# Three 1 MB stores split into 124 and 4 partitions, in a kernel for the gradients of one-query attention

## The chip, the cores and the metric

One core of one Trainium2 chip. The metric is the device time of one execution in microseconds (us); lower is better. Runs whose core shows the usual clock are called fast runs and only these are compared. Every comparison has runs of the kernel before on the same chip beside it.

## The reference, cut to what matters

```python
B, H, Sq, Skv, Dh = 1, 32, 1, 8192, 128            # all bfloat16

def _fwd_reference(q, k, v):
    scores = jnp.einsum('bhqd,bhkd->bhqk', q, k) * q.shape[-1] ** -0.5
    attn = jax.nn.softmax(scores, axis=-1)
    return jnp.einsum('bhqk,bhkd->bhqd', attn, v)

def reference(q, k, v, grad_out):
    out, vjp = jax.vjp(_fwd_reference, q, k, v)
    return (out, *vjp(grad_out))                    # out, dQ, dK, dV
```

With one query per head, K and V (2 MB a head each) are read once, and dK and dV (2 MB a head each) are written once. That is 134 MB in and 134 MB out. dV of a head is an outer product: p (8192 numbers) times grad_out (128 numbers).

## The kernel before

All large transfers are issued by one queue (SP). A tile has 128 partitions; partition p holds 64 neighbouring rows of the sequence, so that half a tile of dK or dV is one contiguous piece of 8 KB a partition. K and V are loaded whole, with 16 KB a partition. dK and dV are written in halves of 1 MB:

```python
    def rows_of(x, h, c, parts):
        L = NT // parts
        return x[0, h].rearrange("(p n) d -> p n d", p=P)[:, c * L:(c + 1) * L, :]

    def load_k(h):
        Kt[h] = kpool.tile([P, NT, D], BF16, tag="K", name="Kt")
        parts = NCH if h == 0 else 1
        for c in range(parts):
            nc.sync.dma_start(slots(Kt[h], c, parts), rows_of(k, h, c, parts))
    # ... load_v is the same with V
    # ... outer(h, which, r): quarter r of dK or dV of head h
        nc.vector.tensor_tensor(slots(G, r, 4)..., op=ALU.mult)
        parts = 4 if h == H - 1 else NST            # NST = 2
        if r % (4 // parts) == 4 // parts - 1:
            c = r // (4 // parts)
            nc.sync.dma_start(rows_of(dst, h, c, parts), slots(G, c, parts))
    # ... the loop over heads, cut to the order of the transfers
    for h in range(H + 1):
        p_ = h - 1
        # ... load_v(h + 1); ds_of(p_); outer(p_, "dk", 0); dq_of(p_, 0)
        if h > 0:
            dq_of(p_, 1)
            outer(p_, "dk", 1)                      # stores the first half of dK
        if 0 < h and h + 2 < H:
            load_k(h + 2)
        # ... outer(p_, "dk", 2), outer(p_, "dk", 3): second half of dK; then both halves of dV of h
```

## Time and profile before

| kernel before | value |
|---|---|
| median of 3 runs | 667.95 us (667.87 to 668.68) |
| busiest compute engine | 77% (PE, DVE) |
| share of the span in which the 16 transfer engines had packets of the large transfers | 97.0% |
| bytes moved, from the page | 134 MB read and 134 MB written |

The prediction below shows the lines of the profile that this rests on: the engine line, the row of GB/s in 40 slices of the span, the share of the large queue, the chain of waits, three stretches of time, the waits of the issuing queue and the landing times of the transfers.

### The profile page before, as it was taken

The numbers are of one execution on the slowest core, as the hardware profiler recorded it, in microseconds if no ns is written. First come the engines' busy times: TensorE is split into PE (matmuls) and PEld (weight loads), VectorE is DVE, ScalarE is ACT, GpSimd is POOL, SyncE is SP. The second block draws the span as 40 slices with busy tenths as digits, with TensorE's granted clock in tenths as the row PEclk, the third lists the DMA queues.
The fourth block names the chain that finished last, engine by engine and source line by source line (L and its number), as shares of the span: only waits on it lengthen the run. The fifth ranks groups of instructions, "written<-read, shape, count | busy, mean of one in ns | idle before, by whom it ended". The sixth has DMA issues, their size and how long they took to land.

```text
span 667.0 us, 23105 instructions
## 1 busy us (share of the span) xinstructions
PE 516.8 (77%) x10727; PEld 485.8 (73%) x10727; DVE 512.5 (77%) x658; ACT 182.1 (27%) x321; POOL 0.7 (0%) x6
## 2 busy tenths in 40 slices
PE   2887988888887777878779787787776888778881
PEld 1887878878877767877668676677766777677870
DVE  4797888888877797777877778777788776887762
ACT  0333323232323222232222322223312223223230
POOL 0000000000000000000000000000000000000000
PEclk9995556566565565555555655666557665555555
DMA  8999999999999999999999999999999999999783
GB/s 330 414 425 424 419 427 414 424 423 426 425 425 424 425 425 424 425 429 423 423 427 426 423 416 422 413 412 418 395 423 418 397 416 406 409 420 403 270 357 142
DMA packets 29807, 269.94 MB, mean 405 GB/s; under 512 B 3472, under 2 KB 3472, under 8 KB 6032
## 3 DMA queue, kind: packets, MB, share of 16 engines
q1 hardware_dynamic: 29712, 268.48, 97.0%
q8 instruction: 83, 1.36, 0.7%
q14 instruction: 12, 0.10, 0.0%
HBM read 134.23 MB, written 134.23 MB: 403 GB/s over the span
## 4 chain that ended last, share of the span: by engine, by line
DMA 75%; PE 17%; DVE 3%; ACT 2%; issue 1%; SPq 0%; ACTq 0%
DMA Kt<-in_k_dram 26%; DMA Vt<-in_v_dram 26%; DMA out_dram<-G_dv 23%; PE T_ps L168 7%; PE s_ps L145 2%; PE dp_ps L185 2%; PE m_ps L185 2%; PE dp_ps L180 1%; DVE XK_sb L133 1%; ACT XT_sb L170 1%; PE m_ps L255 1%; DVE G_dk L195 1%; PE m_ps L268 1%; PE s_ps L161 0%; ACT qd L211 0%
## 5 line engine op out<-in xcount | busy, mean ns | idle before, releaser
L168 PE MATMUL T_ps<-ident,Vt 128*128 128x128 bf16 x2048 | 228.7, 302 | 31.9 <-DMA Vt<-in_v_dram 31.9
L168 PEld LDWEIGHTS <-Vt 128*128 128x128 bf16 x2048 | 201.1, 142 | 33.8 <-DMA Vt<-in_v_dram 33.6
L133 DVE STREAM_TRANSPOSE XK_sb<-Kt 128x1024 f32<-128x1024 f32 x128 | 148.2, 1213 | 81.1 <-DMA Kt<-in_k_dram 81.1
L170 ACT COPY XT_sb<-T_ps 128x1024 f32<-128x1024 f32 x128 | 129.5, 1012 | 189.7 <-PE T_ps L168 189.7
L195 DVE TENSOR_TENSOR G_dk<-ds_rep,qd 128x2048 bf16<-128x2048 bf16 x128 | 155.7, 1219 | 1.1
L195 DVE TENSOR_TENSOR G_dv<-p_rep,qd 128x2048 bf16<-128x2048 bf16 x128 | 148.2, 1220 | 8.5 <-ACT p_rep L277 8.5
L180 PEld LDWEIGHTS <-XT_sb 128*128 128x128 bf16 x2048 | 74.7, 106 | 27.2 <-ACT XT_sb L170 27.2
L180 PE MATMUL dp_ps<-doT,XT_sb 128*128 128x1 bf16 x2048 | 73.6, 166 | 24.4 <-ACT XT_sb L170 24.4
L145 PE MATMUL s_ps<-q_blk,XK_sb 128*128 128x4 bf16 x2048 | 59.1, 168 | 23.2 <-DVE pdt L216 20.5
L145 PEld LDWEIGHTS <-XK_sb 128*128 128x128 bf16 x2048 | 56.5, 103 | 25.5 <-DVE pdt L216 22.3
L185 PE MATMUL dp_ps<-ds_rep,Kt 128*128 128x1 bf16 x2048 | 64.7, 165 | 6.6 <-issue 6.0
L185 PEld LDWEIGHTS <-Kt 128*128 128x128 bf16 x2048 | 59.9, 104 | 12.3 <-issue 12.3
L185 PEld LDWEIGHTS <-Vt 128*128 128x128 bf16 x2048 | 61.1, 105 | 0.0
L185 PE MATMUL m_ps<-p_rep,Vt 128*128 128x1 bf16 x2048 | 60.5, 166 | 0.0
L226 ACT COPY dq_all<-dp_ps 128x1 f32<-128x1 f32 x32 | 5.1, 159 | 173.9 <-PE dp_ps L185 173.9
L268 PEld LDWEIGHTS m_ps<-rs,ones_f 128*128 128x128 f32 x64 | 16.0, 310 | 48.6 <-ACT e L267 48.6
L268 PE MATMUL m_ps<-rs,ones_f 128*128 128x1 f32 x64 | 18.7, 360 | 39.2 <-ACT e L267 39.2
L264 DVE TENSOR_REDUCE nbias<-m_ps 128x1 f32<-128x128 f32 x32 | 9.3, 292 | 22.0 <-ACT qd L211 22.0
L255 PE MATMUL m_ps<-diag,ones_f 128*128 128x128 f32 x64 | 25.3, 499 | 0.7 <-DVE diag L253 0.7
L218 DVE SCALAR_TENSOR_TENSOR ds_rep<-dp_ps,pdt,p_s 128x256 bf16<-128x256 f32 x32 | 15.5, 484 | 12.0 <-PE dp_ps L180 9.6
L277 ACT ACTIVATE p_rep<-e,rinv 128x256 bf16<-128x256 f32 x32 | 16.2, 507 | 30.3 <-DVE rinv L275 30.3
L211 ACT CAST qd<-m_ps 128x256 bf16<-128x256 f32 x32 | 11.9, 372 | 42.4 <-PE m_ps L207 42.4
(40 smaller groups left out, 163.0 us busy)
## 6 DMA issues: line engine op xcount, KB each, us to landing
Kt<-in_k_dram SPq DMA_DIRECT2D x31, 2048.0 KB, 28.0
out_dram<-G_dv SPq DMA_DIRECT2D x62, 1024.0 KB, 25.8
out_dram<-G_dk SPq DMA_DIRECT2D x62, 1024.0 KB, 28.0
Vt<-in_v_dram SPq DMA_DIRECT2D x30, 2048.0 KB, 28.3
Vt<-in_v_dram SPq DMA_DIRECT2D x8, 512.0 KB, 13.8
Kt<-in_k_dram SPq DMA_DIRECT2D x4, 512.0 KB, 5.4
out_dram<-G_dv SPq DMA_DIRECT2D x4, 512.0 KB, 16.9
out_dram<-G_dk SPq DMA_DIRECT2D x4, 512.0 KB, 10.7
```

Of the source, the lines that this page charges most:

```text
L133: nc.vector.transpose(XK[h][:, :, :, u, :], slots(Kt[h], u, NCH).rearrange("p g d -> p (g d)").bitcast(F32).rearrange("p (g w j) -> p g w ...
L145: nc.tensor.matmul(out[:, g, :], lhsT=cols[:, g, c // 2, c % 2], rhs=q_blk[:, h, c, :], start=(c == 0), stop=(c == 2 * NB - 1), skip_group ...
L168: nc.tensor.transpose(T_ps[:, i, :], Vt[h][:, c * CH + i, :], ident[:])
L170: nc.scalar.copy(X.rearrange("p c s -> p (c s)").bitcast(F32), T_ps.rearrange("p c s -> p (c s)").bitcast(F32))
L180: nc.tensor.matmul(st[h]["dp"][:, n:n + 1], lhsT=X[:, i, :], rhs=doT[:, h:h + 1], start=True, stop=True, skip_group_check=True)
L185: nc.tensor.matmul(out_col, lhsT=Xt[:, n, :], rhs=rep[:, n, 0:1], start=(n == 0), stop=(n == NT - 1), skip_group_check=True)
L195: nc.vector.tensor_tensor(slots(G, r, 4).rearrange("p n (a b) -> p n a b", b=R), slots(rep, r, 4).unsqueeze(2).to_broadcast([P, Q, D // R, ...
L211: nc.scalar.copy(x["qd"][:].rearrange("p a d -> p (a d)"), x["m"][:, 256:512])
L218: nc.vector.scalar_tensor_tensor(out=x["ds"][:], in0=x["dp"][:, 0:NT].unsqueeze(2).to_broadcast([P, NT, R]), scalar=pdt[:], in1=x["p_s"][: ...
L255: nc.tensor.matmul(x["m"][:, 128:256], lhsT=ones_f[:], rhs=diag[:], start=True, stop=True, skip_group_check=True)
L268: nc.tensor.matmul(x["m"][:, 0:1], lhsT=ones_f[:], rhs=rs[:], start=True, stop=True, skip_group_check=True)
L277: nc.scalar.activation(x["p"][:], e[:].unsqueeze(2).to_broadcast([P, NT, R]), ACT.Copy, scale=rinv[:])
```

## The change

The store of the second half of dV of heads 8, 16 and 24 is cut into 124 and 4 partitions. Point 1 of the prediction says how many engines a transfer uses: as many, up to 16, as divide its partitions. Both pieces, of 124 (4 x 31) and of 4: four engines. So the other twelve have nothing to do in this store. The intent: if one of the twelve sets the end of the kernel, it gets three stores less.

```diff
+SHIFTED = (8, 16, 24)
...
         if r % (4 // parts) == 4 // parts - 1:
             c = r // (4 // parts)
-            nc.sync.dma_start(rows_of(dst, h, c, parts), slots(G, c, parts))
+
+            cuts = (0, P - 4, P) if which == "dv" and h in SHIFTED and c == 1 else (0, P)
+            for lo, hi in zip(cuts, cuts[1:]):
+                nc.sync.dma_start(rows_of(dst, h, c, parts)[lo:hi], slots(G, c, parts)[lo:hi])
```

In what follows, "shifted store" is a store cut in this way.

## The prediction

> **What bounds the kernel now.** I read the page first: engines, slices, chain. The engine lines and the chain:
>
> ```profile
> PE 516.8 (77%) x10727; PEld 485.8 (73%) x10727; DVE 512.5 (77%) x658; ACT 182.1 (27%) x321; POOL 0.7 (0%) x6
> ...
> GB/s 330 414 425 424 419 427 414 424 423 426 425 425 424 425 425 424 425 429 423 423 427 426 423 416 422 413 412 418 395 423 418 397 416 406 409 420 403 270 357 142
> ...
> q1 hardware_dynamic: 29712, 268.48, 97.0%
> ...
> DMA 75%; PE 17%; DVE 3%; ACT 2%; issue 1%; SPq 0%; ACTq 0%
> ```
>
> No compute engine is above 77%, while the data queue has packets in flight for 97.0% of 16 engines' span and the chain that ended last is DMA for 75%. So transfers set the time. The second thing to see is the slope inside the GB/s row: 425 in the first half, 395 to 420 later, with nothing new in the program. The stretches confirm it (columns: stretch, length, busy us of PE, PEld, DVE, ACT, POOL, clock, DMA share, GB/s):
>
> ```profile
> 150.00:250.00 100.00, 81.24 (x1679) 76.39 (x1677) 81.27 (x102) 28.25 (x50) 0.00 (x0) 0.57 1.01 426
> ...
> 450.00:550.00 100.00, 75.90 (x1606) 71.67 (x1607) 76.50 (x95) 27.78 (x49) 0.00 (x0) 0.60 1.01 411
> 550.00:610.00 60.00, 47.58 (x941) 44.72 (x938) 45.57 (x58) 16.95 (x30) 0.00 (x0) 0.53 1.01 413
> ```
>
> Same share, fewer bytes: packets take longer late in the run. Then the issuing queue's waits and the issues:
>
> ```profile
> SPq L203 <- DMA out_dram<-G_dk: 111.7, 52, 2.5
> SPq L203 <- DMA Kt<-in_k_dram: 110.8, 26, 5.2
> SPq L75 <- DMA Vt<-in_v_dram: 97.5, 23, 4.5
> ```
>
> ```profile
> Kt<-in_k_dram SPq DMA_DIRECT2D x31, 2048.0 KB, 28.0
> out_dram<-G_dv SPq DMA_DIRECT2D x62, 1024.0 KB, 25.8
> ```
>
> A store of dK or dV (L203) has no data reason to wait for a load of K. In the trace's issue records only eight completion semaphores are used in turn, so issue n waits until issue n-8 has landed everywhere. Eight issues are about 11 MB, hence some 28 us from issue to landing though 1 MB moves in 2.5 us.
>
> That is an average over 16 engines. The views don't part them, so I took the trace's own records: each transfer's semaphore gets 16 increments, one per engine, each with its time. For a dV store issued at 274.7 us the 16 landings lie, after the first at 286.2 us: seven within 2.6 us, eight from 5.9 to 8.0 us, one at 14.3 us. At 19 us of the run the spread was 0.8 us; at 445 us it is 20.5 us and then stays between 20 and 22. So three kinds of engine exist:
> - seven fast ones;
> - eight that lose about 1.5 us at each 16 KB instruction block: one block took 1009 ns and the packet after it 1106 ns in place of 611; following back-to-back packets, these blocks go round eight engines, about one in 55 us each;
> - one slow one, which gets no such blocks but whose 8 KB packets (stores) take about 315 to 390 ns instead of 309.
>
> The slow engine sets the time. It always has work; the other fifteen run ahead of it until the window of eight issues is used up (445 us), and then wait for it, which is the falling GB/s. At the end it is still alone: the last large store landed on the first engine at 658.3 us and on the last at 665.7 us.
>
> **What the Trainium skill says.**
> 1. "DMA: Bandwidth & Descriptors", section "Why a DMA increments its semaphore by 16 and not by 1": a transfer uses the largest number of engines up to 16 that divides its slowest dimension, and on this issue path the lowest-numbered ones. 128 partitions give 16 (the trace has 16 landings for each transfer); 124 = 4 x 31 gives 4, and 4 gives 4. So both pieces, and not only the small one, move on engines 0 to 3. No transfer of the kernel before uses fewer than 16, so its trace can't show it.
> 2. Same page, "Latency and other measured facts": engines 7 and 15 are usually slower than the rest in traces. The page blames a path that this kernel doesn't use and calls that a guess. The trace agrees that one engine is slower, but doesn't tell its number.
> 3. "Runtime: NRT & Kernel Launch", "Instruction fetch mechanics": each sequencer refills its instruction memory by its own DMA queue in 16 KiB blocks. The trace agrees: 83 packets, 1.36 MB on the instruction queue.
> 4. "SBUF — State Buffer", "Door 1: The DMA port swizzle": a port serves eight given partitions; in a 128-partition transfer each engine has a port to itself. With 31 partitions on one engine that is no longer so. No run so far shows what it costs.
>
> **The change part by part.** Arithmetic, buffers and the instructions of PE, DVE and ACT stay. SP has three more issues, 0.4 us each, on an engine that mostly waits: nothing. The three affected stores, 1 MB each, are at heads 8, 16 and 24.
> - *Off engines 4 to 15:* eight 8 KB packets per store. On a fast engine 8 x 305 ns (309 less 4 of overlap) = 2.44 us; on the slow one 8 x 0.33 = 2.65 us. Three stores: 7.3 and 7.9 us.
> - *Onto engines 0 to 3:* 31 + 1 packets instead of 8, so 24 more: 24 x 305 ns = 7.3 us per store, 22.0 us for three.
> - *The balance.* The slow engine loses (14.3 - 0.8) us over the 267 us from 19 to 286 us, 5.1%. Unthrottled that is, at 640 us, 0.8 + 0.051 x 621 = 32 us behind a fast one (estimate). Engines 0 to 3, if fast, end 22.0 us behind a fast one; the slow engine ends 32 - 7.9 = 24 us behind. So it stays the last, just, and the end moves with its own work: 667.95 - 7.9 = 660.0 us.
> - *In between.* After head 8 (about 180 us) engines 0 to 3 are 7.3 us back, about where the slow one is. After head 24 (about 510 us) they are 22.0 us back and the slow one about 0.8 + 0.051 x 490 - 7.9 = 18 us: for a while they land last, but they have a window of 20 us in front of them, so the slow engine doesn't starve.
> - *Pieces on foreign ports.* While engines 0 to 3 work off the shifted megabyte, the others mostly load (V, then half a dK store, then K), so reads of one port meet seldom. I add 1 us. That gives 661 us. The tail moves with the slow engine, whose backlog lasts to the end.
>
> **The rivals.**
> - *Engines 0 to 3 are among the eight with instruction blocks.* These are about 7.2 us back at 286 us, 2.7%, so 16 to 17 us at 640 us. Plus 22.0 that is 38.5 us against the 32 us of the slow engine now: about 6 us longer, 674 us. Against it: three stores is just the number that balances fast engines against the slow one (7.3n = 32 - 2.65n gives n = 3.2), while for this group it would be under two; whoever chose three seems to have had fast engines. For it: eight of sixteen engines have the blocks, and nothing numbers them. I give it 1 in 5.
> - *Engines 0 to 3 include the slow one, or all 16 are equally the bound.* Then 22 us are added in full: 690 us, 3.3% slower. It is what anyone gets who takes the mean of 97% for every engine. The spread of landings speaks against equality; the page's 7 and 15 against the slow one being below 4. 1 in 10.
> - *A new wait eats the gain.* The load of V after a shifted store lands late because engines 0 to 3 land late, or ports collide heavily: engines 0 to 3 have only about 2 us in hand at the end, so a collision cost of 2 us per store would make them the last engines, at 664 to 668 us. Likely enough to widen the range upward.
> - *More than counted.* If what slows the slow engine is tied to the stores themselves, it gains more than 8 us; beyond 11 us engines 0 to 3 take over, so under 656 us is hard to reach.
>
> **Range and chances.** Some two chances in three lie between 657 and 667 us, around 661; the fetch-group rival at 674 is to be held too, so the range is 657 to 675 us. Faster by over 2% means under 654.6 us, for which both sides of the balance would have to be wrong: 3%. Slower by over 2% means over 681.3 us, the second rival and some unknown: 12%. Within 2%: 85%.
>
> **What would show it.** Right: GB/s stays at about 425 for longer than before and the late stretch 450 to 550 us is above 411; the spread of landings grows to 20 us later than 445 us; each 124-partition store has landings from four engines only and takes about 9.5 us of their time; the last landing on the last engine comes some 7 us earlier. Wrong: the spread of the landings jumps up by 7 us at each of heads 8, 16 and 24 and never falls (then engines 0 to 3 were not ahead); or 8 KB packets of 500 ns and more around these stores (ports); or 16 landings for a 124-partition store (then nothing moved and the time stays at 668).

## The result, and the profile after

| | median | lowest to highest | fast runs |
|---|---|---|---|
| before | 667.91 us | 667.60 to 668.68 | 4 |
| after | 674.65 us | 673.50 to 675.67 | 4 |

The ratio is 1.0099, with a 95% interval of 1.0077 to 1.0120. A ratio is always the mean time of one kernel's fast runs over that of the other's of the same rounds, so it is not quite the ratio of the medians. The outputs of both kernels are correct. The kernel became 6.7 us slower where a gain of 7 us had been forecast.

The page of the kernel after, in the same parts as shown of before:

```profile
PE 511.6 (76%) x10727; PEld 480.9 (71%) x10727; DVE 512.4 (76%) x658; ACT 182.1 (27%) x321; POOL 0.7 (0%) x6
...
GB/s 333 417 421 422 428 418 424 425 422 427 426 403 409 422 425 426 425 426 424 430 404 386 347 428 421 430 425 423 425 429 340 358 292 422 425 423 424 315 405 159
...
q1 hardware_dynamic: 29688, 268.48, 96.1%
...
DMA 70%; PE 20%; DVE 5%; ACT 2%; issue 1%; SPq 0%; ACTq 0%
```

The compute engines have the same work. What is new is three dips in GB/s, one after each shifted store: slight in slices 12 and 13, and deep in 21 to 23 and in 31 to 33. Between them the rate is 420 to 430, also late in the run, where before had fallen to 395 to 420. So the slow decline is gone, and something worse has come in two places.

The same stretches (columns as before: stretch, length, busy us of PE, PEld, DVE, ACT and POOL, clock, DMA share, GB/s), after:

```profile
150.00:250.00 100.00, 80.24 (x1634) 75.48 (x1633) 79.09 (x100) 27.63 (x50) 0.00 (x0) 0.57 1.01 419
330.00:400.00 70.00, 45.55 (x978) 42.60 (x975) 47.08 (x61) 16.43 (x30) 0.00 (x0) 0.60 0.96 392
450.00:550.00 100.00, 69.73 (x1462) 64.95 (x1459) 73.87 (x94) 24.09 (x46) 0.00 (x0) 0.55 0.93 379
550.00:610.00 60.00, 47.44 (x1001) 44.50 (x999) 44.58 (x58) 16.90 (x30) 0.00 (x0) 0.56 1.01 422
```

And the second one of before, which the prediction doesn't show:

```profile
330.00:400.00 70.00, 56.57 (x1157) 53.62 (x1156) 52.03 (x65) 20.08 (x34) 0.00 (x0) 0.53 1.01 423
```

423 GB/s became 392 around the second shifted store, and the DMA share fell under 1: engines stand empty. The prediction had said that the stretch 450 to 550 would be above the 411 of before if it was right. It is 379.

Who stands empty, and why, is in the waits of the issuing queue (total us, times, longest us): the whole run after, then the stretch 330 to 400 alone, then the corresponding line of before.

```profile
SPq L82 <- DMA out_dram<-G_dv: 69.4, 23, 12.4
```

```profile
SPq L82 <- DMA out_dram<-G_dv: 14.4, 2, 12.4
```

```profile
SPq L81 <- DMA out_dram<-G_dv: 55.8, 25, 2.9
```

L82 is the load of V. It waits eight issues behind a shifted store. The longest such wait grew from 2.9 to 12.4 us: the shifted store lands so late that the window of eight issues is used up. In this time the issuing queue starts nothing, and the engines that are ahead run dry.

The issues after, with KB each and the median us from issue to landing on all engines:

```profile
out_dram<-G_dv SPq DMA_DIRECT2D x59, 1024.0 KB, 24.4
...
out_dram<-G_dv SPq DMA_DIRECT2D x3, 992.0 KB
...
out_dram<-G_dv SPq DMA_DIRECT2D x3, 32.0 KB
```

Three stores of 992 KB and three of 32 KB are there. They have no landing time since the view wants 16 landings. In the records, each of the six has landings from four engines.

### The landings, engine by engine

The views don't part the engines, so I worked the following from the trace's landing records. For each transfer of 128 partitions I added up what one engine had been given by all such transfers so far, at 305 ns per 8 KB (the short stores of 124 and 4 and the eight 512 KB loads at the start are left out), and subtracted this sum from each landing time. An engine that does nothing else and never pauses stays at its number. An engine that works a shifted store off rises by the full cost of that store. The fast group rises only if it has to pause. The records don't name an engine, so engines are followed by their place in the order. Shown are the first engine and the last five (us).

```
                        first | the last five
before, near 176 us      15.2 | 19.8 19.9 20.1 20.5 23.9
        near 372 us      15.4 | 24.3 24.4 24.4 26.4 35.0
        near 544 us      24.0 | 30.5 31.3 32.7 33.4 45.1

after,  near 176 us      14.9 | 19.6 19.7 20.1 20.4 22.7     before the first shifted store
        near 203 us      14.9 | 24.7 27.1 28.1 29.9 30.4     after it
        near 332 us      15.0 | 27.2 28.2 30.6 31.1 31.4
        near 364 us      19.8 | 31.6 37.9 40.1 45.3 46.0     after the second
        near 505 us      29.0 | 37.8 39.6 40.2 47.3 48.6
        near 536 us      35.5 | 39.3 53.2 53.6 61.0 63.1     after the third
```

Before, one engine drifts away from the rest, 23.9 to 45.1: the slow one. After, four others rise in three steps, and the slow one (24.7, 31.6, 37.8, 39.3) isn't among them and ends in front of them. Before the first step none of the four stood out. Seven engines stood in front of the others then (within 1.1 us), and three are left there after it: the four come from the front group. So engines 0 to 3 are four of the seven fast ones, and the slow engine is elsewhere, just as the prediction had taken it.

But each step is 14.5 to 15.5 us for the last of the four, from about 15 to 30.4, 31 to 46.0 and 48.6 to 63.1, where 32 packets x 305 ns = 9.8 us had been taken. Between the steps the last engine hardly moves (46.0 to 48.6 in 140 us): it is never without work. It is the one that sets the end.

The packets show the same. 8 KB packets of the large queue that took 420 ns or more, and by how much they exceeded 309 ns in sum, in the 40 us around each shifted store:

```
                    180-220 us        340-380 us        500-540 us
before              2,  0.8 us        6,  2.2 us        4,  1.6 us
after              48, 16.8 us       22,  9.0 us       30, 12.0 us
```

In before such packets are next to absent. In after they take 9 to 17 us in each place, which is 2 to 4 us for each of four engines, if all of them belong to engines 0 to 3; a packet's record doesn't name its engine. The landings allow a check: by the table, the four engines together rise by some 54 to 56, 48 and 55 us at the three stores, which is 15 to 17, 9 and 16 us above 4 x 9.8. That is near the excess of the slow packets at the first two and 4 us more at the third. Of the 48, 14 took 590 to 625 ns, twice the usual time; the longest took 1366 ns.

### The profile page after: what moved, and what is told of

Its sections match the earlier page's. It is cut to its first block, busy times and chain, and to the rows that moved or that the text cites. A ratio compares the mean times of both kernels' runs of the same rounds, so it can differ in the third digit from the quotient of the medians.

```text
span 673.6 us, 23111 instructions
## 1 busy us (share of the span) xinstructions
PE 511.6 (76%) x10727; PEld 480.9 (71%) x10727; DVE 512.4 (76%) x658; ACT 182.1 (27%) x321; POOL 0.7 (0%) x6
## 4 chain that ended last, share of the span: by engine, by line
DMA 70%; PE 20%; DVE 5%; ACT 2%; issue 1%; SPq 0%; ACTq 0%
DMA Kt<-in_k_dram 31%; DMA Vt<-in_v_dram 25%; DMA out_dram<-G_dv 11%; PE T_ps L169 8%; DMA out_dram<-G_dk 4%; DVE XK_sb L134 3%; PE s_ps L146 3%; PE dp_ps L186 2%; PE m_ps L186 2%; PE dp_ps L181 2%; ACT XT_sb L171 1%; PE m_ps L259 1%; DVE G_dk L196 1%; PE m_ps L272 1%; PE s_ps L162 1%
## 5 line engine op out<-in xcount | busy, mean ns | idle before, releaser
L169 PE MATMUL T_ps<-ident,Vt 128*128 128x128 bf16 x2048 | 224.7, 298 | 42.1 <-DMA Vt<-in_v_dram 42.1
L169 PEld LDWEIGHTS <-Vt 128*128 128x128 bf16 x2048 | 197.9, 140 | 43.8 <-DMA Vt<-in_v_dram 43.8
L186 PEld LDWEIGHTS <-Vt 128*128 128x128 bf16 x2048 | 61.1, 105 | 0.0
L272 PEld LDWEIGHTS m_ps<-rs,ones_f 128*128 128x128 f32 x64 | 16.0, 309 | 48.6 <-ACT e L271 48.6
L222 DVE SCALAR_TENSOR_TENSOR ds_rep<-dp_ps,pdt,p_s 128x256 bf16<-128x256 f32 x32 | 15.5, 484 | 11.8 <-PE dp_ps L181 9.6
```

The costliest lines, as they stand in the source:

```text
L169: nc.tensor.transpose(T_ps[:, i, :], Vt[h][:, c * CH + i, :], ident[:])
L186: nc.tensor.matmul(out_col, lhsT=Xt[:, n, :], rhs=rep[:, n, 0:1], start=(n == 0), stop=(n == NT - 1), skip_group_check=True)
L222: nc.vector.scalar_tensor_tensor(out=x["ds"][:], in0=x["dp"][:, 0:NT].unsqueeze(2).to_broadcast([P, NT, R]), scalar=pdt[:], in1=x["p_s"][: ...
L272: nc.tensor.matmul(x["m"][:, 0:1], lhsT=ones_f[:], rhs=rs[:], start=True, stop=True, skip_group_check=True)
```

## The experiments

Theory P: packets of a shifted store meet packets of other engines on ports of the on-chip memory that several engines then share, and so cost more. Rival Q: a 4-engine store costs 9.8 us as worked out, and something else (extra issues, the window of eight, the place in the order) brings the loss. Rival H: what slows it is the memory outside the chip's buffers, or the engines themselves. Which partitions the expectations put on one port is taken from the section that point 4 of the prediction names; the runs test only what that costs. Times before in the runs' own rounds were 667.73 to 668.15 us (medians).

### 1. Stores alone, in several widths

A kernel that is wrong: it fills one tile and stores parts of it, four or eight stores of one kind in a row, with a fill between two kinds.

```diff
-    # the attention kernel
+    full(128, 4); full(124, 4); full(116, 4); full(92, 4); full(76, 4)    # so many stores of so many partitions
+    part(4, 1, 8); part(4, 4, 8); part(4, 32, 8); part(8, 4, 4)           # 4 partitions, at such a step
+    full(119, 4); full(114, 4); full(126, 4); full(120, 4); full(128, 4)
```

> The disputed cost by itself: only stores of one 8 KB-per-partition tile, in stretches parted by a fill of the tile that waits for all stores before it. Results are wrong on purpose. Theory P (packets of engines 0 to 3 meet on SBUF ports): stores of 4 neighbouring partitions, all on one port, take about 1200 ns a packet; 4 partitions at steps of 4, on four ports, 309 ns; 4 partitions at steps of 32, on two ports, about 606 ns. Stores of 124 partitions (31 to an engine, so engine e and e+1 read partitions 31 apart, nearly the same port) take about 606 ns a packet and 4 stores 75 us; stores of 116, 92 and 76 partitions (29, 23, 19 apart) mostly 309 ns, 4 stores 23 to 38 us. Theory Q (four engines alone are slow at writing HBM, or the whole thing is a matter of the other traffic): all these stores have the same mean packet, 309 ns in the quiet, whatever the partitions. Further, stores of 119 (7 engines), 114 (6), 126 (14) and 120 (15) partitions show by packets of 315 to 390 ns which of them include the slow engine.

Measured, 332.28 us in all. The fills of the tile on DVE mark the ends of the kinds (start, us, line, and in brackets the idle time before it):

```profile
17.57 3.47 DVE L57 MEMSET G<- 128x4096 bf16 x1 [12.45 <-issue]
64.08 3.47 DVE L57 MEMSET G<- 128x4096 bf16 x1 [43.03 <-issue]
107.57 3.47 DVE L57 MEMSET G<- 128x4096 bf16 x1 [40.02 <-issue]
```

DVE stands idle for 12.45 us while four stores of 128 partitions go out, 43.03 us for four of 124 and 40.02 us for four of 116. From 128 to 124 that is (43.03 - 12.45) / 4 = 7.6 us a store, and 24 more packets at 305 ns are 7.3 us. In the records the four landings of a 124-partition store are 9.5 to 9.8 us behind those of the store before it, with a mean packet of 324 ns. Theory P as it was put for this run had expected 606 ns and 75 us for the four stores: there it failed. So alone, a 4-engine store costs what I had worked out: what engines 0 to 3 do to each other is not the cause.

But which partitions a store takes does matter. Stores of four partitions, on four engines: neighbours took 478 ns a packet on average, with one of 1165; at a step of 4 partitions 313 ns, none over 400; at a step of 32, 524 ns. Expected were 1200, 309 and 606 ns. So the order of the first two fits shared ports, but neighbours on one port were not slower than a step of 32 on two. Two more findings: other widths land on the number of engines expected from their divisors, and the 16 landings of each of the first four 128-partition stores lie within 0.2 us. In the last four of the run one engine lands 0.6 to 0.9 us after the first. Four stores in a row are too few to tell whether the slow engine is slow when there is nothing but stores.

### 2. and 3. Other cuts at the same heads

```diff
-            cuts = (0, P - 4, P) if ...
+            cuts = (0, 116, P) if ...        # run 2: 116 on 4 engines (29 packets each), 12 on 12 engines
+            cuts = (0, 112, P) if ...        # run 3, control: 112 and 16, both on 16 engines
```

> The same three stores cut as 116 and 12 partitions: 29 + 1 packets on engines 0 to 3 instead of 31 + 1, the 12 on twelve engines. Theory P: partitions 29 apart share a port for a quarter of the packets and not for three quarters, so engines 0 to 3 lose 22 x 0.305 = 6.7 us and at most 2 us of collisions a store; the slow engine stays last at 24 us: 660 to 663 us, packets of 600 ns get rare. Theory Q: the cost goes with the packets, 22/24 of that of the change: 671 to 673 us.

> Control: the same three stores cut as 112 and 16 partitions, which both use 16 engines. Same number of issues and of semaphore uses as the change, but no engine gets other bytes. If the three additional issues in the window of eight cost something: 670 us or more. If only the engines' bytes matter: as before, 667 to 669 us.

Measured: run 2 668.74 us (665.33 to 671.51, six runs), ratio 1.0007 [0.9982, 1.0032]. Run 3 669.03 us (668.41 to 669.52), ratio 1.0015 [1.0003, 1.0027]. The control says that three more issues of the same bytes cost about 1 us: the extra issues aren't the loss. Run 2 met neither expectation. Two fewer packets on engines 0 to 3 at each store save 2 x 305 ns x 3 = 1.8 us by count, and it came out 6 us better than the change, with a spread of 6 us where the kernel before has under 2. The number of packets is the same in every run, so it can't be what spreads. That meetings of packets do is a guess here.

### 4. One shifted store alone

```diff
-SHIFTED = (8, 16, 24)
+SHIFTED = (16,)
```

> Only head 16 is shifted (124 and 4). If the end is that of the engine with the most work, engines 0 to 3 end 12 to 13 us behind a fast engine and the slow one, 32 - 2.65 us behind it, stays last: 665 us, 2.65 us less than before. If each shifted store adds its third of the loss by a stall of its own: 670 us.

Measured: 664.61 us (664.43 to 665.18), ratio 0.9952 [0.9939, 0.9965], as expected. One shifted store is a gain of 3.3 us.

### 5. First probe of a store beside other traffic

As run 1, with a store of 68 or 124 partitions followed by six stores or loads on given partitions.

```diff
+    stretch(68); stretch(68, store=(64, 128)); stretch(68, store=(0, 64))     # other half, same half
+    stretch(68, load=(64, 128)); stretch(68, load=(0, 64))
+    stretch(124); stretch(124, store=(0, 128)); stretch(124, load=(0, 128)); stretch(92, store=(0, 128))
```

> One store on engines 0 to 3 with other traffic behind it in the queues, which engines 4 to 15 start at once. Results are wrong on purpose. Alone, the first probe gave 9.5 us for 124 partitions; so collisions among engines 0 to 3 are not what made it 12 to 13 us in the kernel. Theory P2 (the shifted packets meet, on SBUF ports, the packets of the engines that usually own these ports): the store of partitions 0 to 67 takes 5.2 us alone and beside stores of partitions 64 to 127 (other ports), but 8 us and more beside stores of partitions 0 to 63 (the same ports), with packets of about 600 ns. The store of 124 takes 12 to 13 us beside full stores. Loads write to SBUF; if reads and writes don't share, beside loads it is 9.5 us. Theory H (HBM is the place of the contention): the half of the partitions makes no difference, and full stores or loads slow the store of 68 in both halves alike.

Measured: 302.56 us. Its output is wrong, which doesn't matter for the time. Each following transfer waited for the fill of its own tile, 4.3 us apart, so the traffic was too thin. The 68-partition store took 7.1 to 8.0 us from issue to its landings alone and 7.0 to 8.6 us with any of the four; 124 partitions took 11.7 to 12.8 us alone, 14.0 to 16.4 us with full stores and 12.6 to 14.6 us with full loads. The half-against-half test is inconclusive.

### 6. Two shifted stores, at heads 11 and 21

```diff
+CUTS = {11: (0, 124, 128), 21: (0, 124, 128)}
-            cuts = (0, P - 4, P) if which == "dv" and h in SHIFTED and c == 1 else (0, P)
+            cuts = CUTS.get(h, (0, P)) if which == "dv" and c == 1 else (0, P)
```

> Two shifted stores of 124 and 4 (heads 11 and 21) instead of three. With 12.8 us a store for the slowest of engines 0 to 3: 25.6 us behind a fast engine, against 32 - 5.3 = 26.7 us of the slow one: 662 to 664 us, the slow engine still last or level. If every store cost a stall of its own beyond the engines' sums: 667 us or more.

Measured: 661.50 us (660.87 to 663.30), ratio 0.9906 [0.9891, 0.9921]. Two shifted stores gain 6.2 us in their rounds. So none, one, two and three give 667.9, 664.6, 661.5 and 674.7 us: some 3.2 us less for each of the first two, and then a turn. By the sums of the landings, a single engine is the last one with one shifted store, 10 us behind the next near 640 us (run 4). With two, the last two engines are level at the end (within 0.3 us in this run).

### 7. and 8. Smaller first parts, and a map of the engines

```diff
+CUTS = {8: (0, 92, 128), 16: (0, 92, 128), 24: (0, 92, 128)}                 # run 7: 92 on 4 engines (23 packets each)
+CUTS = {10: (0, 119, 128), 13: (0, 120, 128), 16: (0, 114, 128), 19: (0, 121, 128),
+        22: (0, 100, 128), 25: (0, 63, 128), 28: (0, 115, 128)}              # run 8: on 7, 15, 6, 11, 10, 9 and 5 engines
```

> Three stores cut as 92 (engines 0 to 3, 23 packets) and 36 partitions (12 engines, 3 packets). Engines 0 to 3 get 18 packets more a store, 5.5 us, with collisions 7.5 to 8 us, in all 23 to 24 us; the slow engine, which is among engines 4 to 11, loses 5 packets a store, in all 5 us: 27 us. So 662 to 664 us, faster than before by 0.6 to 0.9%. If the cost of a shifted store doesn't shrink with its packets: 670 us.

> One look, to number the engines: half stores cut so that they use 7, 15, 6, 11, 10, 9 and 5 engines at heads 10, 13, 16, 19, 22, 25 and 28, with remainders on 9, 8, 14, 7, 14, 13 and 13. From which landings have the lag of the slow engine: the skill's page says 7 or 15; the 12-engine store of the 116 and 12 run had it among its landings, so 15 is out. If it is 7, stores on 5, 6 and 7 engines lack it and those on 8 and more have it. If it is one of 4 to 6, the store on 7 has it.

Run 7: 668.04 us (664.81 to 670.24, six runs), ratio 0.9999 [0.9973, 1.0024], a miss by 4 to 6 us and nearer to the 670 us of the other branch. Again the spread is over 5 us. In its records the last of engines 0 to 3 rises by 11 to 15 us at each store for 26 packets (7.9 us at 305 ns). Run 8, one look of unknown state, took 691.91 us. Its stores on 7, 6 and 5 engines seem to include the slow engine, which would make it the fifth in number. That is read off how its lag moves and is not shown.

### 9. Second probe, with the tiles filled first

```diff
-        nc.vector.memset(G[:], val[0])       # ahead of the fills of the other tiles
         for t in T:
             nc.vector.memset(t[:], val[0])
+        nc.vector.memset(G[:], val[0])
```

> Wrong on purpose: stores and loads alone, the store over few engines issued first and six 1 MB transfers right behind it, all their tiles filled beforehand (in the earlier probe of this kind the fills thinned the traffic). Theory P (a slow store is slow because its packets meet packets of other engines on the ports of its own partitions): the store of 68 partitions takes some 7 us from issue to its last landing alone and beside stores or loads of the other 64 partitions, and 9 us or more beside those of the same 64, with packets near 600 ns; 124 partitions beside full stores 13 to 16 us against 11.5 to 12.5 alone. Theory H (memory or the engines themselves): the half makes no difference. If loads delay it as much as stores do, reads and writes share what is short.

Measured: 302.56 us, and no result again. The scheduler that orders the instructions put each following transfer as early as its tile allowed, which was now ahead of the store under test. Where the order within a probe matters, look at the built order, and tie it with data.

### 10. to 12. The load of K moved ahead of the dK store

```diff
             dq_of(p_, 1)
+            if p_ in SWAPPED:
+                load_k(h + 2)
             outer(p_, "dk", 1)
-        if 0 < h and h + 2 < H:
+        if 0 < h and h + 2 < H and p_ not in SWAPPED:
             load_k(h + 2)
+# run 10: SHIFTED = SWAPPED = (8, 16, 24); run 11: shifted and swapped at 11 and 21; run 12: SWAPPED = (8, 16, 24), none shifted
```

> The changed kernel with the load of K moved ahead of the store of the first half of dK at heads 8, 16 and 24, so that V and K are loaded (9.8 us) while engines 0 to 3 work the shifted store off, and no store meets it. Theory P with stores alone meeting stores: the packets of 600 ns around the shifted stores go away, a shifted store takes about 10 us in place of 11.4 to 13.6, and the time is 663 to 667 us. If loads meet it just as well, or the cost is elsewhere: 673 to 676 us, as the changed kernel.

> The best version so far (two shifted stores, heads 11 and 21: 661.5 us) with the same swap of the load of K at these two heads. The slow engine sets the end there by my reading and the swap doesn't change its bytes: 660 to 662.5 us under either theory; over 664 us would mean that the swap costs something by itself.

> Control: the swap of the load of K at heads 8, 16 and 24 in the kernel before, no store shifted. Bytes of each engine are unchanged: 667 to 669 us. If it moves the time by more than 2 us, the run with the swap and the three shifted stores has to be read against this one.

| run | median, us | ratio to before [95%] |
|---|---|---|
| 10, three shifted, swapped | 676.24 (674.72 to 678.82) | 1.0131 [1.0110, 1.0153] |
| 11, two shifted, swapped | 663.34 (662.53 to 663.64) | 0.9929 [0.9915, 0.9942] |
| 12, none shifted, swapped | 668.17 (667.85 to 669.69) | 1.0009 [0.9996, 1.0021] |

The swap is free by itself and didn't help. The excess of the slow packets fell at the first shifted store (16.8 to 10.2 us), where the engines are nearly level, and rose at the second (9.0 to 14.9 us) and the third (12.0 to 16.8 us). "Only stores meet stores" as a way out of the loss has fallen. A likely reason is that at the later stores engines 0 to 3 lag behind the others by more than 10 us, so that what they meet is not what follows them in the order; that was not tested. Why run 11 is 1.8 us above run 6 stays open.

### 13. Third probe, with the order tied by data

The following stores read the same tile as the store under test, and the following loads go to tiles of which a few bytes are copied from it after its fill. The built order: the store under test comes first, and six transfers behind it.

```diff
-                nc.sync.dma_start(half(out_2, out_3)[lo:hi], t[lo:hi])
+                nc.sync.dma_start(half(out_2, out_3)[lo:hi], G[lo:hi])
+        for t in T:
+            nc.vector.tensor_copy(out=t[:, 0:1, 0:2], in_=G[:, 0:1, 0:2])    # after the fill of G
```

> Wrong on purpose: a store over four engines and six transfers right behind it, in an order that copies of a few bytes force, so that this time they do overlap. Theory P (ports of the partitions): the store of 68 partitions (17 packets an engine, 5.2 us of packets, some 7.2 us from issue to last landing) is as quick beside stores of the other 64 partitions as alone, and takes 9 to 12 us beside stores of the same 64, with packets near 600 ns there alone; loads the same if reads and writes share a port. 124 partitions beside full stores: 14 to 17 us against 11.5 to 12.5 alone. Theory H (memory outside or the engines): both halves slow it alike. If neither half slows it, the cost isn't in single stores at all.

Measured (one execution, wrong, 270.6 us), from issue to the landing on the last of the four engines:

| store under test | alone | + stores, other 64 partitions | + stores, same 64 | + loads, other 64 | + loads, same 64 |
|---|---|---|---|---|---|
| 68 partitions | 7.9 us | 8.3 us | 11.5 us | 9.4 us | 9.4 us |

| store under test | alone | + full stores | + full loads |
|---|---|---|---|
| 124 partitions | 12.8 us | 20.4 us | 14.4 us |
| 92 partitions | not run here | 13.2 us | not run |

The timeline carries the same verdict: a fill waits until everything of the stretch before it has landed. Fills of G on DVE (start, us):

```profile
18.96 3.47 DVE L64 MEMSET G<- 128x4096 bf16 x1 [0.92 <-DVE G L63]
...
47.27 3.47 DVE L64 MEMSET G<- 128x4096 bf16 x1 [0.92 <-DVE G L63]
...
78.84 3.47 DVE L64 MEMSET G<- 128x4096 bf16 x1 [0.92 <-DVE G L63]
...
107.67 3.47 DVE L64 MEMSET G<- 128x4096 bf16 x1 [0.92 <-DVE G L63]
...
136.43 3.47 DVE L64 MEMSET G<- 128x4096 bf16 x1 [0.92 <-DVE G L63]
```

The four stretches between these fills are: stores of the other half 28.31 us, stores of the same half 31.57 us, loads of the other half 28.83 us and loads of the same half 28.76 us. The number of bytes is the same in all four. Only stores care which half it is, and they cost 3.2 to 3.3 us in the same half. That is what theory P says of stores. Rival H has fallen as far as it means the load on outer memory or on the engines as a whole: bytes and engines are alike in the two. One gap is left. The rows written in outer memory move with the half too, so a cost that hangs on the address there isn't excluded for stores; for loads, whose rows move in the same way, the half made no difference. Loads delay the store by 1.5 us in either half, which is not a port of these partitions, so P has fallen as far as it spoke of loads. Slow packets were expected beside the same half alone and are in both stretches: between issue and landing of the store under test, 151 of 212 packets took 420 ns or more beside the other half, and 202 of 241 beside the same. The 124-partition store is delayed by 7.6 us by full stores (to 20.4 us, where 14 to 17 had been expected) and by 1.6 us by full loads. In the kernel, where both follow it, the last engine paid some 5 us above 9.8, between the two.

### 14. The third shifted store undone

```diff
-SHIFTED = (8, 16, 24)
+CUTS = {8: (0, 124, 128), 16: (0, 124, 128)}
```

> The changed kernel with its shifted store at head 24 undone: shifted stores at heads 8 and 16 alone. By my account of engines 0 to 3 (about 14 to 15 us of their time for each shifted store, less the 2.4 us that they do anyway) and of the slow engine (3.2 us less for each), the slow engine and engines 0 to 3 are then level: 661 to 664 us. If the places of the first two cost more than those at heads 11 and 21 did, 666 to 670 us.

Measured: 661.47 us (660.64 to 661.90), ratio 0.9897 [0.9881, 0.9914]. The row of GB/s of this kernel:

```profile
GB/s 334 415 424 424 423 421 424 424 424 424 425 412 406 426 425 425 425 426 425 424 410 416 310 416 424 425 428 425 423 425 423 426 427 422 426 423 424 350 399 173
```

The dip after the second shifted store, slices 21 to 23, is there as in the changed kernel, and the long wait of the load of V with it (12.8 us). Still this kernel is 6.7 us faster than before. The dip after the third is gone, and with it 674.65 - 661.47 = 13.2 us. Near 505 us its engines stand as those of the changed kernel do (last five 38.2 38.8 39.8 45.5 47.4), and near 536 us they still do (38.9 39.7 39.9 45.4 47.4), where the changed kernel had 63.1. So the loss is the third store's own cost on engines 0 to 3: a step of 14.5 to 15.5 us less the 2.4 us that they would have had anyway is 12 to 13 us, and 13.2 were measured.

With the two-store versions at heads 8 and 16 (661.47 us) and at heads 11 and 21 (661.50 us), there are two that beat both kernels, by 0.9 to 1.0% against before. Their difference is far inside the runs' spread.

## Why the prediction was right or wrong

- **Transfers bound it, and three kinds of engine exist.** Right. Compute has no new work, and the landings of after part as they did before.
- **124 partitions go on four engines, which are among the fast ones; the slow engine isn't one of them.** Right: four landings, from engines of the front group. The rival at 674 us has the right number by chance: its reason, that engines 0 to 3 fetch instruction blocks, is not what the landings show.
- **Off the slow engine: 2.65 us per store.** Nearly right: 3.3 us in run 4, where it still ends last. Runs 6 and 14 gained 6.2 and 6.7 us with two, but there engines 0 to 3 are level with it or last, so they don't measure it.
- **The slow engine is 32 us behind at 640 us, and the others run into the window at 445 us.** Both a little off: the spread of the landings had reached 20.9 us near 394 us already, and in the sum of the landings the slow engine ends 35 us behind where the fast group stood before it paused.
- **Onto engines 0 to 3: 7.3 us per store, 22.0 us for three, with 1 us in all for pieces on foreign ports ("reads of one port meet seldom").** This is the step that failed. Run 1 shows that 7.3 us is right for a store alone (7.6 us). In the kernel the step is 14.5 to 15.5 us on the last of the four engines, so 12 to 13 us above what it would have had. Three times this is 36 to 39 us in place of 23. The balance "22 against 24" is thereby lost at the third store. With the prediction's own start (the slow engine 32 us behind a fast one at 667.95, so that a fast one would end near 636), engines 0 to 3 end at 672 to 675 us. 674.65 was measured. That it fits so well is partly luck: the 35 us above would put this end 3 us earlier, and the last engine lost some 5 us more between the steps.
- **Why it failed.** Two sentences of the prediction hold the gap. It knew that ports are shared and that engines 0 to 3 had only 2 us in hand, and named collisions of 2 us a store as a rival at 664 to 668 us. It then sized them at 0.3 us without a measurement, and the rival too was sized at less than half of the 5 us that came. Shown: a store is delayed more beside stores of the same partitions than beside stores of others (run 13, 11.5 us against 8.3 us), and packets of twice the usual time lie around the shifted stores of the kernel. That the delay is a shared port, and that these packets in the kernel are the same meetings, is inferred. No run takes the meetings away from the kernel and leaves the rest; run 10 tried and failed.
- **"They have a window of 20 us in front of them, so the slow engine doesn't starve."** Wrong in its number: the four were up to 28 us behind, and the issuing queue stood for 12.4 us. This cost the other twelve engines time that they had to spare. Run 14 has the stall at the second store too and is still faster, and the last engine never ran dry. So the wait is a result of the late engines and not the cause of the loss.
- **What would show it.** The signs that the prediction listed did their work: four landings (right), 9.5 us of their time (right alone, wrong in the kernel), the late stretch above 411 (wrong: 379), and packets of 500 ns and more around the stores (named as the sign of ports; there they are). One sign needs care: if the landings' spread jumped by 7 us at each shifted store and never fell, engines 0 to 3 were not to have been ahead. By the table it did jump, by 8 to 10 us each time, though they had been ahead; it was the second half that failed, since it fell again (from 26 to 20 us between the second and the third).

## What to carry to other kernels

Moving bytes from a late engine to early ones pays until the early ones become the last, so try one, two and three before settling; the best of those tried is two. A transfer on few engines costs its packet count only while nothing else moves: beside stores of the same partitions it took nearly 60% longer (12.8 to 20.4 us, one execution), so size it in the traffic in which it will run. A margin of 2 us in a balance of 22 against 24 us is no margin for a term that has not been measured.

## What the Trainium skill lacked or had wrong

- "DMA: Bandwidth & Descriptors": its rule for the number of engines held (124 partitions gave 4 landings, 119 gave 7, 114 gave 6). It doesn't say what a store on few engines costs beside other traffic: 20.4 us beside full stores and 14.4 us beside full loads, against 12.8 us alone.
- The same page names engines 7 and 15 as the slow ones. Here one engine is slow, and a look at stores on 5 to 7 engines suggests the fifth; that is an inference from one run. Whether the slowness is the engine's own is open: with nothing but stores the 16 landings lay within 0.2 us in four stores and one came 0.6 to 0.9 us after the first in four others.
- "SBUF — State Buffer", section "Door 1: The DMA port swizzle": its table agrees in part: neighbours (one port by the table) 478 ns a packet against 313 ns at a step of 4 (four ports), and 11.5 us against 8.3 us for stores of the same and of the other half. But a step of 32, two ports by the table, took 524 ns, no less than one port. The page lacks that loads delay a store independently of the half, by 1.5 us.
- No page says that stores on few engines can make a kernel's time scatter: 5 to 6 us from run to run with 92 or 116 partitions on four engines, against under 2 us in the kernel before.
